# Start bytes of TensorE's operands in the second layer, and a first chunk of 510 columns

## The chip, the core and the metric

The kernel runs on one core of a Trainium2 chip. The metric is the time of one execution on the device in microseconds; the text gives the median of several runs and, for its reasoning, the one execution that the profiler recorded.

## What is computed

The reference takes x (2 x 3008 x 256), makes the real part of its Fourier transform over the last two axes, and sends the 6016 rows through two layers, each with its own weights of 256 x 2048 and 2048 x 256:

```
X = fft(fft(x, axis=1), axis=2).real              # 6016 rows of 256
h = X @ w_in;  g = h * sigmoid(h);  y = g @ w_out                # layer one
h = y @ w_in2; g = h * clip(h + 3, 0, 6) / 6; out = g @ w_out2   # layer two
```

## The kernel before, in words

The transform comes first, as three steps of small matmuls (function names step1, step2, step3). Because x is real, rows come in pairs: a pair of rows is one column of a table `eo` that holds the even and the odd part, and there are 3010 pairs (`NPAIR`, 2 x 1505). The table is cut along its columns into six **chunks** (lines 52 to 56): the first has 512 columns, the other five 500 each, together `NCOL` = 3012. The last two columns are padding; line 429 sets them to zero. All that follows is done chunk by chunk, so a matmul streams 500 or, in the first chunk, 512 columns.

**Precision.** Every product in float32 is made of three matmuls on float32r halves (`mm3`, lines 302 to 305): the high half of the weights times the high half of the moving operand (line 303), high times low (line 304), low times high (line 305). Each matmul has a weight load of its own. So weights exist as `whi` and `wlo`, hidden values as `ghi` and `glo`, and so on.

**Layer one** (`win1`, `win1_end`, `wout1`). For each chunk and each of 16 blocks of 128 hidden units: two products into `ab` (6 matmuls) and four products into the accumulators `y` (12 matmuls), 18 matmuls in all. The two layers' outputs between them go to DRAM (`y1_d`) and come back as `u`.

**Layer two** (the loop over `units2` at the end of `body`). The first product of the layer is done with seven products in place of eight on pairs of blocks. The seven moving operands are made by `moving` from `u`, in this order: b11, b21, t1, t2, t4, t3, b22. The seven products are at lines 888, 889, 897, 910, 923, 925 and 939; in the profile they read `pa<-b` (b11), `pc<-b` (b21), `pb<-t` (t1), `pa<-t,wx` (t2), `pd<-t` (t4), `pa<-t,whi` (t3) and `pb<-b` (b22). The weights of b11, b21, t4 and t3 come from `whi` and `wlo`, those of t1, t2 and b22 from `wx`, sums of weights that `load_w2` (line 264) loads. Then `wout2` makes eight products into `y`. A unit is one pair of blocks of a chunk: 7 x 3 + 8 x 3 = 45 matmuls; a chunk has eight units. Chunk 1 has its pass between the two halves of chunk 0, chunks 2 to 5 follow, and a product's accumulation runs a little behind.

**Where operands lie.** Every operand tile has rows of 512 words (`LINE`), so each half starts at the same byte modulo 512 as its tile; only the number of columns streamed differs. The tiles come from pools at these addresses (bytes in a partition):

- weights of both layers (`wp`, from 8,448 on): 256 modulo 512
- hidden values `ghi`, `glo` (right side of the memory): 448
- the ring of operands (line 687): 10 slots, `x0` to `x9`. Slots 0 to 3 lie in `xsp`, on the right side (from 184,256 on): 448. Slots 4 to 9 lie in `xq` (line 615; from 114,944 on): 256. The counter starts at slot 4, and each pass takes seven slots in the order of the operands above. Chunk 0 is taken twice, so the passes are chunk 0, 1, 0, 2, 3, 4, 5.
- `wx` (line 266): it takes the place of `eo` at 204,736: 448

In layer one moving operands lie in `xsp` (448) and weights in `wp` (256). Right-side pools are laid from the top of the memory downwards; the topmost slot is the one that `eo` and `wx` share, 24,608 bytes, set by the larger of the two.

The order of the work is written out by hand in `body`: the program order on each engine is the order of the calls. Loads and stores go through SP's queue, some stores of layer one through POOL's.

Of the kernel before, what the change touches and what calls it, by code (L numbers as in the profile page):

```python
# [36 lines left out]
F32 = mybir.dt.float32  # L37
F32R = mybir.dt.float32r
# [8 lines left out]
NPAIR = B * (S // 2 + 1)  # L47
SELF = NB // 2 + 1
HALFB = NPAIR // B
FF, P = 2048, 128  # L50
NF = FF // P
NCOL = 3012
CHUNK = 512
LINE = 512
CHUNKS = [(max(0, 500 * j + 12), 500) for j in range(6)]
CHUNKS[0] = 0, CHUNK


NJ = NB // 4
# [24 lines left out]
def body(tc, xh, x128, t1, t2, t3, w1, w128, w2, out):  # L84
    nc = tc.nc
    V, A, T, G = nc.vector, nc.scalar, nc.tensor, nc.gpsimd
# [4 lines left out]
    eop = tc.alloc_tile_pool(name="eop", bufs=1, side="right")  # L91
# [3 lines left out]
    three, mask, minus, warm = (consts[:, i : i + 1] for i in range(4))  # L95
    eo = eop.tile([P, 2, NCOL], F32, name="eo", tag="eo")
    w2_d = [
        [dr.tile([P, 2, n], F32, name=f"w2{q}_d{g}", tag=f"w2{q}_d{g}") for q, n in (("h", 512), ("l", 512), ("x", 384))]
        for g in range(NF // 2)
    ]  # L100
    e128_d = [dr.tile([1, n], F32, name=f"e128_d{j}", tag=f"e128_d{j}") for j, (_, n) in enumerate(CHUNKS)]
    x_d = [[dr.tile([P, 2, n], F32, name=f"x{h}_d{j}", tag=f"x{h}_d{j}") for h in "hl"] for j, (_, n) in enumerate(CHUNKS)]
    y1_d = [dr.tile([P, 2, 2 * n], F32, name=f"y1_d{j}", tag=f"y1_d{j}") for j, (_, n) in enumerate(CHUNKS)]

# [34 lines left out]
    def weight_tiles(key, g):  # L139
        whi[key, g] = wp.tile([P, 2, 512], F32R, name=f"whi{key}_{g}", tag=f"whi{g}")  # L140
        wlo[key, g] = wp.tile([P, 2, 512], F32R, name=f"wlo{key}_{g}", tag=f"wlo{g}")
# [69 lines left out]
    wx = []  # L211
# [51 lines left out]

    def load_w2(g):
        if not wx:
            flat = eop.tile([P, NF * 384 + 8], F32R, name="wx", tag="eo")[:, : NF * 384]
            wx.append(flat.rearrange("p (g i c) -> p g i c", i=2, c=384))
        weight_tiles(2, g)
        for dst, src in zip((whi[2, g], wlo[2, g], wx[0][:, g]), w2_d[g]):
            nc.sync.dma_start(dst.bitcast(F32), src)  # L270
# [155 lines left out]
        return c + 256  # L426

    V.memset(three, 3.0)
    V.memset(eo[:, :, NPAIR:], 0.0)
    G.memset(nil, 0.0)  # L430
    cleared = (V, ((2, 0, 1), (2, 2, 3), (3, 0, 2))), (G, ((2, 1, 2), (2, 3, 4), (3, 2, 4), (4, 0, 4), (5, 0, 4)))
    for eng, slots in cleared:
# [74 lines left out]
    def split_eo(k, j):  # L507
        c, n = CHUNKS[j]
        hi, lo = (xsp.tile([P, 2, LINE], F32R, name=f"x{h}{k}", tag=f"x{2 * (k % 2) + i}") for i, h in enumerate(("hi", "lo")))
        eb = xsp.tile([P, LINE], F32, name=f"eb{k}", tag="eb", bufs=2)  # L510
        new = k < len(CHUNKS)
        if new:
            nc.sync.dma_start(e128_d[j], eo[0:1, 1, c : c + n])
        nc.sync.dma_start(eb[:, :n], e128_d[j].to_broadcast([P, n]))
        if new:
            split(hi[:, :, :n], lo[:, :, :n], eo[:, :, c : c + n], x_d[j])
        else:
            for x, d in zip((hi, lo), x_d[j]):
                nc.sync.dma_start(x[:, :, :n].bitcast(F32), d)
        return hi, lo, eb  # L520
# [93 lines left out]
    stp = tc.alloc_tile_pool(name="stp", bufs=1, reuse_waits="tile")  # L614
    xq = tc.alloc_tile_pool(name="xq", bufs=1, reuse_waits="tile")
    psB = tc.alloc_tile_pool(name="psB", bufs=1, space=PSUM, reuse_waits="tile")
    kept, ys = {}, {}

    def low(k, f, shared=False):
# [129 lines left out]
    for i in range(n1):  # L749
        k, f = units[i]  # L750
        j, fs = segs[k]
# [29 lines left out]
        if not odd and 0 <= q < FIRST + 1:  # L781
            load_w2(q)
# [92 lines left out]
    for e, (k, f) in enumerate(units2):  # L875
        j, fs = segs2[k]
# [64 lines left out]
        if e < half - FIRST - 1:  # L941
            load_w2(FIRST + 1 + e)
# [146 lines left out]
```

## Time and profile before

| | |
|---|---|
| median of 3 runs | 923.89 us (923.83 to 923.91) |
| the profiled execution | 923.64 us |
| its span, first to last instruction | 921.5 us |
| PE busy, share of the span | 915.9 us, 99% |
| DVE, ACT, POOL busy | 661.9, 649.6, 527.3 us |
| matmuls | 4286 |

PE is TensorE's matmuls, PEld its weight loads, DVE VectorE, ACT ScalarE, POOL GpSimd, SP the queue of SyncE. Matmuls are pipelined: a recorded duration reaches from a matmul's start to its modelled end and overlaps the next one, so what counts on PE is the distance from one start to the next.

### The profile page before, as it was taken

How to read it: one execution, taken by the hardware profiler on the slowest of the kernel's cores; microseconds unless marked ns; L12 is line 12 of the kernel's file. 1: busy time of each engine (PE TensorE's matmuls, PEld its weight loads, DVE VectorE, ACT ScalarE, POOL GpSimd, SP SyncE). 2: the span in 40 equal slices, each digit the busy share in tenths (PEclk: the TensorE clock that was granted, in tenths of full speed). 3: DMA queues.
4: the chain of work that ended last, by engine and by line, in shares of the span. 5: the costliest groups of instructions: out<-in, count | busy, mean ns of one | idle time of the engine just before them, and what ended most of it. 6: DMA issues, size and time to landing. Idle time of an engine off the chain costs nothing.

```text
span 921.5 us, 12152 instructions
## 1 busy us (share of the span) xinstructions
PE 915.9 (99%) x4286; PEld 775.2 (84%) x4286; DVE 661.9 (72%) x908; ACT 649.6 (70%) x1144; POOL 527.3 (57%) x391
## 2 busy tenths in 40 slices
PE   9999999999999999999999999999999999999998
PEld 8988888888888888888888888888888888888886
DVE  7989999989899999985564565565555555555544
ACT  4878767666767666677776778666776777677665
POOL 2065646745465665554775577745765675576553
PEclk9999999999999999999999999999999999999999
DMA  8554344043272726696230002020020002001001
GB/s 323 195 209 158 136 146 143 6 143 145 85 207 92 220 93 163 188 371 198 107 90 1 1 1 90 0 91 1 1 90 0 1 1 90 1 1 45 1 1 44
DMA packets 28744, 89.32 MB, mean 97 GB/s; under 512 B 2886, under 2 KB 14667, under 8 KB 25644
## 3 DMA queue, kind: packets, MB, share of 16 engines
q1 hardware_dynamic: 26796, 81.85, 24.9%
q0 software_dynamic: 1504, 6.17, 3.7%
q8 instruction: 33, 0.54, 0.2%
q10 hardware_dynamic: 384, 0.54, 0.2%
q14 instruction: 27, 0.22, 0.1%
HBM read 52.33 MB, written 36.22 MB: 96 GB/s over the span
## 4 chain that ended last, share of the span: by engine, by line
PE 98%; DVE 1%; DMA 0%; ACT 0%; issue 0%; SPq 0%
PE y L303 18%; PE y L304 18%; PE y L305 18%; PE ab L303 5%; PE ab L304 5%; PE ab L305 4%; PE pa L303 4%; PE pa L304 4%; PE pa L305 4%; PE pb L305 2%; PE pb L303 2%; PE pb L304 2%; PE ps L368 1%; PE ps L411 1%; PE pd L304 1%; PE pc L303 1%
## 5 line engine op out<-in xcount | busy, mean ns | idle before, releaser
L806 POOL TENSOR_TENSOR glo<-h,ghi 128x500 fp32r<-128x500 f32 (+1 forms) x191 | 246.4, 1302 | 186.7 <-ACT ghi L803 182.7
L624 POOL TENSOR_TENSOR glo<-h,ghi 128x500 fp32r<-128x500 f32 (+1 forms) x137 | 211.8, 1559 | 190.9 <-ACT h L583 182.3
L303 PE MATMUL y<-ghi,whi 128*128 128x500 f32 (+1 forms) x768 | 295.7, 385 | 0.0
L304 PE MATMUL y<-glo,whi 128*128 128x500 f32 (+1 forms) x768 | 295.6, 385 | 0.0
L305 PE MATMUL y<-ghi,wlo 128*128 128x500 f32 (+1 forms) x768 | 295.4, 385 | 0.0
L303 PEld LDWEIGHTS y<-ghi,whi 128*128 128x128 f32 x768 | 144.3, 188 | 27.3
L305 PEld LDWEIGHTS y<-ghi,wlo 128*128 128x128 f32 x768 | 144.2, 188 | 27.0
L304 PEld LDWEIGHTS y<-glo,whi 128*128 128x128 f32 x768 | 144.2, 188 | 26.9
L803 ACT ACTIVATE ghi<-h 128x500 fp32r<-128x500 f32 (+1 forms) x192 | 118.0, 624 | 47.9 <-DVE h L798 46.6
L582 ACT ACTIVATE ghi<-ab 128x500 fp32r<-128x500 f32 (+1 forms) x96 | 56.4, 587 | 87.2 <-DVE h L573 85.4
L798 DVE SCALAR_TENSOR_TENSOR h<-h,pc 128x500 f32<-128x500 f32 (+1 forms) x96 | 65.1, 678 | 71.5 <-ACT h L795 71.5
L928 DVE TENSOR_TENSOR pc<-u,pb 128x500 f32<-128x500 f32 (+1 forms) x48 | 32.9, 685 | 109.5 <-ACT u L864 109.5
L795 ACT ACTIVATE h<-pc,consts 128x500 f32<-128x500 f32 (+1 forms) x96 | 64.6, 673 | 40.4 <-DVE pc L928 36.0
L864 ACT ACTIVATE u<-pa 128x500 f32<-128x500 f32 (+1 forms) x96 | 56.6, 589 | 51.7 <-PE pa L305 48.4
L303 PE MATMUL ab<-xhi,whi 128*128 128x500 f32 (+1 forms) x192 | 74.4, 387 | 0.2 <-DVE st L562 0.2
L304 PE MATMUL ab<-xlo,whi 128*128 128x500 f32 (+1 forms) x192 | 74.0, 386 | 0.0
L305 PE MATMUL ab<-xhi,wlo 128*128 128x500 f32 (+1 forms) x192 | 73.8, 384 | 0.0
L562 DVE SCALAR_TENSOR_TENSOR st<-eb,w_sb,ab 128x500 f32<-128x500 f32 (+1 forms) x92 | 67.0, 728 | 8.3 <-PE ab L305 8.3
L573 DVE SCALAR_TENSOR_TENSOR h<-st,ab 128x500 f32<-128x500 f32 (+1 forms) x92 | 61.3, 667 | 7.8 <-PE ab L305 7.7
L798 DVE SCALAR_TENSOR_TENSOR h<-h,pd 128x500 f32<-128x500 f32 (+1 forms) x96 | 64.4, 671 | 1.2 <-ACT h L795 1.2
L795 ACT ACTIVATE h<-pd,consts 128x500 f32<-128x500 f32 (+1 forms) x96 | 64.6, 673 | 0.5 <-DVE pd L940 0.5
L583 ACT ACTIVATE h<-h 128x500 f32<-128x500 f32 (+1 forms) x96 | 60.0, 625 | 3.0
(166 smaller groups left out, 1576.2 us busy)
## 6 DMA issues: line engine op xcount, KB each, us to landing
raw<-in_w SPq DMA_DIRECT2D x16, 1024.0 KB, 6.9
y_d<-st SPq DMA_DIRECT2D x5, 1000.0 KB, 5.1
y_d<-st POOLq DMA_DIRECT2D x5, 1000.0 KB, 8.0
u<-y_d SPq DMA_DIRECT2D x5, 1000.0 KB, 5.3
out<-st SPq DMA_DIRECT2D x19, 250.0 KB, 2.2
w2h_d<-h SPq DMA_DIRECT2D x8, 512.0 KB, 2.6
w2l_d<-t SPq DMA_DIRECT2D x8, 512.0 KB, 3.2
whi<-w2h_d SPq DMA_DIRECT2D x8, 512.0 KB, 5.8
```

What stands on the lines that cost most here:

```text
L303: T.matmul(o, wh, xhi, start=first, stop=False, **group)
L304: T.matmul(o, wh, xlo, start=False, stop=False, **group)
L305: T.matmul(o, wl, xhi, start=False, stop=last, **group)
L562: V.scalar_tensor_tensor(out=z[:, :n], in0=eb[:, :n], scalar=w128_sb[:, f : f + 1], in1=ab[:, :n], op0=ALU.mult, op1=ALU.add)
L573: V.scalar_tensor_tensor(out=h[:, 0, :n], in0=z[:, :n], scalar=2.0, in1=ab[:, :n], op0=ALU.mult, op1=ALU.subtract)
L583: A.activation(h[:, s, :n], src, AF.Silu)
L624: eng.tensor_tensor(out=glo[:, s, :n], in0=h[:, s, :n], in1=ghi[:, s, :n], op=ALU.subtract)
L795: A.activation(h[:, i, :n], c[:, :n], AF.Relu, bias=three)
L798: V.scalar_tensor_tensor(out=h[:, i, :n], in0=h[:, i, :n], scalar=6.0, in1=c[:, :n], op0=ALU.min, op1=ALU.mult)
L803: A.activation(g[0][:, i, :n], h[:, i, :n], AF.Copy)
L806: E.tensor_tensor(out=g[1][:, i, :n], in0=h[:, i, :n], in1=g[0][:, i, :n], op=ALU.subtract)
L864: A.activation(t[:, :n], pa[:, :n], AF.Copy)
```

## The change

The chunks cover exactly the 3010 pairs: the first has 510 columns in place of 512, the others begin two columns earlier, and the padding and its memset go. The slot of `wx` gets 128 words more, and `wx` starts 80 words (320 bytes) into it. A tile of 48 words (192 bytes) that nobody uses stands at the head of `xq`.

```
-NCOL = 3012
+NCOL = 3010
 CHUNK = 512
 LINE = 512
-CHUNKS = [(max(0, 500 * j + 12), 500) for j in range(6)]
-CHUNKS[0] = 0, CHUNK
+CHUNKS = [(max(0, 500 * j + 10), 500) for j in range(6)]
+CHUNKS[0] = 0, 510
...
     def load_w2(g):
         if not wx:
-            flat = eop.tile([P, NF * 384 + 8], F32R, name="wx", tag="eo")[:, : NF * 384]
+            flat = eop.tile([P, NF * 384 + 136], F32R, name="wx", tag="eo")[:, 80 : 80 + NF * 384]
...
     V.memset(three, 3.0)
-    V.memset(eo[:, :, NPAIR:], 0.0)
     G.memset(nil, 0.0)
...
     psB = tc.alloc_tile_pool(name="psB", bufs=1, space=PSUM, reuse_waits="tile")
+    xq.tile([P, 48], F32, name="gap", tag="gap")
```

## Rows read from the trace of the kernel before

**Rows 1.** The page, its first lines: the span, and each engine's busy time.
```profile
span 921.5 us, 12152 instructions
## 1 busy us (share of the span) xinstructions
PE 915.9 (99%) x4286; PEld 775.2 (84%) x4286; DVE 661.9 (72%) x908; ACT 649.6 (70%) x1144; POOL 527.3 (57%) x391
```
**Rows 2.** The page, the chain that ended last, shares of the span by engine.
```profile
PE 98%; DVE 1%; DMA 0%; ACT 0%; issue 0%; SPq 0%
```
**Rows 3.** Waits of PE, longest: us in total, times, longest us.
```profile
PE psw L351 <- POOL nil L430: 1.0, 1, 1.0
```
**Rows 4.** Windows in layer 2: length, then busy us (records that overlap) by engine.
```profile
core 0: us, PE busy (x) PEld busy (x) DVE busy (x) ACT busy (x) POOL busy (x), PEclk, DMA share, GB/s
481.80:549.00 67.20, 67.20 (x304) 56.70 (x303) 36.49 (x58) 46.99 (x80) 38.78 (x30) 1.00 0.01 5
603.80:671.20 67.40, 67.40 (x304) 56.84 (x303) 38.08 (x60) 46.54 (x79) 38.52 (x30) 1.00 0.07 24
```
**Rows 5.** Timeline of PE in layer 1: start us, duration us; eight matmuls between.
```profile
300.02 0.38 PE L304 MATMUL ab<-xlo,whi 128*128 128x500 f32 x1
...
302.00 0.38 PE L304 MATMUL y<-glo,whi 128*128 128x500 f32 x1
```
**Rows 6.** Groups by form, 260 to 370 us (layer 1): busy us, mean ns | idle.
```profile
L303 PE MATMUL y<-ghi,whi 128*128 128x500 f32 x112 | 42.8, 382 | 0.0
```
**Rows 7.** Groups by form, 671.2 to 751.2 us (layer 2, chunk 3).
```profile
L304 PE MATMUL y<-glo,whi 128*128 128x500 f32 x64 | 24.6, 384 | 0.0
...
L304 PE MATMUL pd<-t,whi 128*128 128x500 f32 x8 | 3.1, 390 | 0.0
...
L304 PE MATMUL pc<-b,whi 128*128 128x500 f32 x8 | 3.1, 382 | 0.0
```
**Rows 8.** Groups by form, 831 to 911 us (layer 2, chunk 5).
```profile
L304 PE MATMUL pc<-b,whi 128*128 128x500 f32 x8 | 3.1, 390 | 0.0
...
L304 PE MATMUL pd<-t,whi 128*128 128x500 f32 x8 | 3.1, 382 | 0.0
```
**Rows 9.** Timeline of PE in layer 2: starts at the edges of passes.
```profile
481.67 0.38 PE L303 MATMUL pb<-t,wx 128*128 128x500 f32 x1
...
549.13 0.39 PE L303 MATMUL pa<-b,whi 128*128 128x512 f32 x1
...
603.73 0.39 PE L303 MATMUL pb<-t,wx 128*128 128x500 f32 x1
...
671.26 0.39 PE L303 MATMUL pa<-b,whi 128*128 128x500 f32 x1
...
751.19 0.39 PE L303 MATMUL pa<-b,whi 128*128 128x500 f32 x1
...
830.98 0.39 PE L303 MATMUL pa<-b,whi 128*128 128x500 f32 x1
...
910.95 0.39 PE L303 MATMUL y<-ghi,whi 128*128 128x500 f32 x1
```
**Rows 10.** Groups by form, whole span: matmuls of 512 columns.
```profile
L305 PE MATMUL y<-ghi,wlo 128*128 128x512 f32 x128 | 50.6, 396 | 0.0
L303 PE MATMUL y<-ghi,whi 128*128 128x512 f32 x128 | 50.6, 395 | 0.0
...
L304 PE MATMUL pa<-t,whi 128*128 128x512 f32 x8 | 3.2, 398 | 0.0
...
L303 PE MATMUL pa<-t,whi 128*128 128x512 f32 x8 | 3.1, 390 | 0.0
```
**Rows 11.** Groups by form, around 173 us: the first and second 512-wide matmul after 500-wide ones.
```profile
L304 PE MATMUL ab<-xlo,whi 128*128 128x512 f32 x1 | 0.4, 398 | 0.0
L303 PE MATMUL ab<-xhi,whi 128*128 128x512 f32 x1 | 0.4, 387 | 0.0
```
**Rows 12.** Timeline of DVE at the start: start us, duration us, [idle before].
```profile
0.85 0.06 DVE L429 MEMSET eo<- 128x4 f32 x1
...
4.17 0.43 DVE L339 TENSOR_TENSOR x<-x 128x256 f32<-128x256 f32 x1 [0.82 <-DMA x<-in_xh]
```
**Rows 13.** DMA issues: KB each, median us to landing.
```profile
out<-st SPq DMA_DIRECT2D x4, 256.0 KB, 2.1
```

## The prediction

> **What bounds the kernel now.** I read the page's engine shares first, then the chain, then the waits of PE. PE is busy 915.9 of 921.5 us, the chain that ends last is PE for 98% of it, and the longest single wait of PE in the whole run is 1.0 us at the start [rows 1, 2, 3]. So the time is the sum of the steps from one matmul's start to the next, and everything else runs beside it. A change can pay here only by fewer matmuls, narrower ones, or a shorter step for the same width.
>
> The windows by stage show the other engines: in a 67.4 us stretch of layer 2 ACT is busy 46.5 us, POOL 38.5 and DVE 38.1, with the granted clock at 1.00, the 2.4 GHz level [rows 4]. None of them is near PE.
>
> Now the step itself. The timeline of a layer-1 stretch has starts at 300.02 and, nine matmuls later, at 302.00: 0.220 us a step for 500 columns [rows 5]. The same matmuls are listed with a duration of 382 ns [rows 6]: durations overlap, so I read a row's step as its duration less 162 ns. In layer 1 every row of that stretch says 382.
>
> In layer 2 they don't, and the rows tell why. Take two passes with the same code, weights and width. From 671 to 751 us the product pd (operand t4) takes 390 ns and pc (operand b21) 382 [rows 7]; from 831 to 911 us it is the other way round, pd 382 and pc 390 [rows 8]. What differs is the slot of the operand. The ring starts at slot 4 and takes seven slots a pass, so in the first of these passes b21 is in slot 3 (xsp, byte 448 of 512) and t4 in slot 6 (xq, byte 256); in the second b21 is in slot 7 (xq) and t4 in slot 0 (xsp). Their weights lie at 256. A product whose operand and weights start at the same byte of 512 is slow; one with 448 against 256 is not. Neighbours pay as well: y, always 448 against 256, is at 384 in this pass and at 382 in layer 1 [rows 6, 7].
>
> **The change, part by part.** *Layer 2, 500 columns.* The 48-word tile puts xq at 114,944 + 192 = 115,136, which is 448 modulo 512. The slot of wx grows from 24,608 to 25,120 bytes, so the pools of the right side all move down by 512 and keep their 448, and wx starts at 204,224 + 320 = 204,544, which is 256. Then every matmul of layer 2 has the pairing of layer 1, and I give it layer 1's 0.220 us. What this removes comes from starts. A unit has 45 matmuls, a pass of eight units 360. From 671.26 to 910.95 are three passes: 239.69 us against 1080 x 0.220 = 237.60, an excess of 2.09 [rows 9]. From 481.67 to 549.13 and from 603.73 to 671.26 there are 303 each (the windows list 304, one of which began earlier [rows 4]): 67.46 and 67.53 against 66.66, an excess of 0.80 and 0.87 [rows 9]. That is 3.76 us over 1686 matmuls; the other 114 of the 1800 are mixed with wider ones, and at the same rate hold 0.25. **Term: -4.0 us**, with 3.5 to 4.3 as its bounds (without the 114, and less some that stays at the joints; or a little more at the joints).
>
> *First chunk, 510 columns.* It has 16 x 18 = 288 matmuls in layer 1 and 360 in layer 2. At 512 columns y and ab have about 395.4 ns, a step of 233.4; the 168 products of layer 2 lie between 398 and 390, about 393, a step of 231 [rows 10]. So here the pairing hardly matters. And width is not smooth: the first 512-wide matmul after a run of 500 takes 387, just 5 ns for 12 columns (0.42 ns each), but the next one 398 [rows 11]. No row has 510. From below, it is 220 + 10 x 0.42 = 224.2 a step, if a run of 510 stays on that first step. From above, it is the costliest of 512, 398 - 162 = 236. I take the nearest row, 512, less two columns: 233.4 - 0.8 = 232.6. For 288 + 192 matmuls that is 0.8 ns less, -0.40 us; for the 168 products, which now all have the other pairing and which I let go to the same 232.6, +0.27. **Term: -0.13 us**, between -5.6 (480 x 9.2 + 168 x 6.8 ns) and +2.1 (480 x 2.6 + 168 x 5.0 ns).
>
> *The rest.* The memset of the padding is 0.06 us on DVE, which afterwards waits 0.82 us for the first input anyway [rows 12]: nothing; without that cover 0.06 us. The first chunk's transfers lose two columns in 512 (its stores of 256 KB land in 2.1 us, on SP's queue [rows 13]); PE waits for no DMA in either layer, so nothing. No step is moved, no wait is added. If PE gets faster, the next engine in layer 2 is ACT, busy for 46.5 of 67.4 us [rows 4], and 303 steps of 0.220 still take 66.7: nothing becomes late.
>
> **Sum.** -4.0 - 0.13 = -4.13 on the profiled execution of 923.64 us (span 921.5 and 2.1 around it): 919.5. The median of the runs is 0.25 above the profiled one, so 919.8.
>
> **Rivals.** *The first chunk goes cheap.* With 510 columns the step stays near 224.2 to 229. For: the lone 512-wide matmul at 387. Against: every longer run of 512 is 8 ns above that. By its end the time is 923.9 - 4.0 - 5.6 = 914.3. The Trainium skill, "TensorE: Matmul & The Clock Gate", section Back-to-back issue gap, has the gap grow by one cycle per column, so by that page this rival would hold; the row at 387 agrees with it, and the rows at 395 do not.
>
> *Addresses are not the cause.* Something else that differs between the passes makes the 390s, and only two columns in 648 matmuls go: 648 x 0.83 ns = 0.54 us, 923.35, no measurable change. Against: pd and pc swap places exactly with their slots. The Trainium skill, "SBUF — State Buffer", section Who interferes with whom, gives PE two independent read ports, one for the moving operand and one for weights, and says that "PE and ACT never wait on anyone"; by that page the start bytes could not matter and this rival would hold. The rows with 390 and 382 for one line speak against it.
>
> *Slower: 510 is a bad width.* 510 columns are 2,040 bytes, no multiple of 16, where 500 and 512 are. If each such matmul pays another step of the size that the rows show between 387 and 398, it is 648 x 11 ns = 7.1 us: 923.9 - 4.0 + 7.1 = 927.0. It decides from 4.0 / 648 = 6.2 ns a matmul on. For: the price of width is visibly uneven. Against: no row shows an odd price for a width that isn't a multiple of something.
>
> *The layout doesn't come out as stated*, say wx is moved but the ring is not: then products only trade places, and the time stays at about 923. Against: the addresses above follow from the tile sizes.
>
> **Chances.** Forecast (first chunk between 229 and 236 a step) 0.66; cheap first chunk 0.20; addresses not the cause 0.07; bad width 0.04; layout 0.03. A change of 0.2%, 1.85 us, is about what a measurement can tell. The forecast and the cheap chunk lie below 922.04, but for the forecast's last edge; so faster 0.85, same 0.10, slower 0.05. The range takes the two ends of the unknown width, 914.3 to 923.9 - 4.0 + 2.1 = 922.0; it leaves out the last three cases, 0.14.
>
> **What would show it.** Right: from the second chunk on, all products of layer 2 and y at 382 in every pass, and three passes in 237.6 us. For the first chunk, rows of 510 near 394 to 395; 386 to 387 means the cheap rival, above 400 the bad width. Wrong: pd or pc still at 390 in some pass, or layer-2 steps that lengthen with new waits of PE on ACT or DVE.

## The result, and the profile after

The changed kernel takes 916.35 us (median of 4 runs, 916.08 to 916.56) against 923.9 before: a ratio of 0.9918, 95% interval 0.9901 to 0.9935, 7.55 us less. The profiled execution took 916.08 us, its span is 914.0 [before: rows 1]. The text had forecast 919.8 with a range of 914.3 to 922.0.

The page's first lines after. PE is still the whole span; it has the same 4286 matmuls.
```profile
span 914.0 us, 12150 instructions
## 1 busy us (share of the span) xinstructions
PE 908.0 (99%) x4286; PEld 774.4 (85%) x4286; DVE 664.1 (73%) x907; ACT 649.6 (71%) x1144; POOL 528.3 (58%) x391
```
Groups by form of the whole span: first the 500-wide `y`, then `y` and two products of the first chunk, now 510 wide.
```profile
L303 PE MATMUL y<-ghi,whi 128*128 128x500 f32 x640 | 244.5, 382 | 0.0
...
L304 PE MATMUL y<-glo,whi 128*128 128x510 f32 x128 | 49.8, 389 | 0.0
...
L304 PE MATMUL pa<-t,whi 128*128 128x510 f32 x8 | 3.1, 389 | 0.0
...
L303 PE MATMUL pa<-t,whi 128*128 128x510 f32 x8 | 3.1, 388 | 0.0
```
The same view for the pass of chunk 3, 665.8 to 745 us, where pd and pc had changed places with their slots [rows 7, 8]:
```profile
L304 PE MATMUL pc<-b,whi 128*128 128x500 f32 x8 | 3.1, 382 | 0.0
...
L304 PE MATMUL pd<-t,whi 128*128 128x500 f32 x8 | 3.1, 382 | 0.0
```
And the timeline of PE at the first and last edge of the three last passes [rows 9]:
```profile
665.84 0.38 PE L303 MATMUL pa<-b,whi 128*128 128x500 f32 x1
...
903.44 0.38 PE L303 MATMUL y<-ghi,whi 128*128 128x500 f32 x1
```
The three passes take 903.44 - 665.84 = 237.60 us, exactly 1080 steps of 0.220, where they took 239.69. In these passes the excess of layer 2 at 500 columns is gone as forecast. The first chunk is the surprise: its rows stand at 389, a step of 227, where 512 columns had 395 and the forecast 394 to 395.

A little was given back. Around the start of the pass of chunk 1 some steps are long. The timeline of PE, two places:
```profile
466.23 0.38 PE L305 MATMUL pa<-b,wlo 128*128 128x500 f32 x1
466.49 0.50 PE L303 MATMUL pc<-b,whi 128*128 128x500 f32 x1
466.83 0.39 PE L304 MATMUL pc<-b,whi 128*128 128x500 f32 x1
...
470.70 0.39 PE L303 MATMUL pd<-t,whi 128*128 128x500 f32 x1
471.02 0.50 PE L304 MATMUL pd<-t,whi 128*128 128x500 f32 x1
471.36 0.39 PE L305 MATMUL pd<-t,wlo 128*128 128x500 f32 x1
```
Steps of 0.26, 0.34, 0.32 and 0.34 us in place of 0.22 are 0.4 us in these four alone. What PE waited for there stands in the timelines of DVE and POOL:
```profile
465.75 0.69 DVE L798 SCALAR_TENSOR_TENSOR h<-h,pc 128x510 f32<-128x510 f32 x1 [0.22 <-ACT h L795]
...
469.68 2.50 POOL L693 TENSOR_TENSOR t<-u,t 128x500 fp32r<-128x500 f32 x2
```
The matmul at 466.49 overwrites pc, which DVE had read until 466.44. The one at 471.02 takes the low half of t4, the first of the two that POOL made from 469.68 on; it was done just before. Over all long steps from 465 to 476 us the excess is 0.67 us, where the same work had 0.20 in the kernel before.

### The profile page after: what moved, and what is told of

The parts are those of the page before. It is cut to its first block, busy times and chain, and to the rows that moved or that the text cites. A ratio compares the mean times of both kernels' runs of the same rounds, so it can differ in the third digit from the quotient of the medians.

```text
span 914.0 us, 12150 instructions
## 1 busy us (share of the span) xinstructions
PE 908.0 (99%) x4286; PEld 774.4 (85%) x4286; DVE 664.1 (73%) x907; ACT 649.6 (71%) x1144; POOL 528.3 (58%) x391
## 4 chain that ended last, share of the span: by engine, by line
PE 98%; DVE 1%; DMA 0%; ACT 0%; issue 0%; SPq 0%
PE y L305 18%; PE y L303 18%; PE y L304 18%; PE ab L303 5%; PE ab L304 5%; PE ab L305 5%; PE pa L303 3%; PE pa L305 3%; PE pa L304 3%; PE pb L303 2%; PE pb L304 2%; PE pb L305 2%; PE ps L368 1%; PE ps L411 1%; PE pd L304 1%; PE pc L303 1%
```

## The experiments

**The two parts alone.** e1 has the new addresses with the old chunks, e2 the new chunks with the old addresses.

```
 e1 (against the changed kernel)
-NCOL = 3010
+NCOL = 3012
-CHUNKS = [(max(0, 500 * j + 10), 500) for j in range(6)]
-CHUNKS[0] = 0, 510
+CHUNKS = [(max(0, 500 * j + 12), 500) for j in range(6)]
+CHUNKS[0] = 0, CHUNK
...
+    V.memset(eo[:, :, NPAIR:], 0.0)

 e2 (against the changed kernel)
-            flat = eop.tile([P, NF * 384 + 136], F32R, name="wx", tag="eo")[:, 80 : 80 + NF * 384]
+            flat = eop.tile([P, NF * 384 + 8], F32R, name="wx", tag="eo")[:, : NF * 384]
...
-    xq.tile([P, 48], F32, name="gap", tag="gap")
```

> The operand addresses of the change, with the chunks of before (first chunk 512 columns with its padding). Theory: the two parts are separate, and the addresses give 4.0 us in layer 2 at 500 columns (every row there at 382 ns), while the 512-wide products lose some 0.4 us since they go to the 233 ns step of the others; about 920.3 us. Rival: the addresses give the whole gain, by way of the first chunk too: about 916.4. Second rival: the gain needs the new width: about 923.

> First chunk of 510 columns, operand addresses as before. Theory: layer 1 at 510 columns steps by 226.7 ns in place of 233, 1.8 us less; in layer 2 the 500-wide rows keep 382 to 390 ns, and the 510-wide ones lie between 226.7 and 231 ns, 0.5 to 2.0 us less; 920.1 to 921.6 us. Rival: the 510 columns run at 226.7 only with the new addresses: about 923.4.

e1 took 920.68 us, a ratio of 0.9966 (0.9955 to 0.9977); e2 920.74, 0.9964 (0.9951 to 0.9977). So each part gives 3.3 us against 923.99 in the same runs; together 6.6, against 7.55 for both at once, which is within the intervals. The rows by form of `y` in e1 say which width each had:
```profile
L303 PE MATMUL y<-ghi,whi 128*128 128x500 f32 x640 | 244.6, 382 | 0.0
...
L303 PE MATMUL y<-ghi,whi 128*128 128x512 f32 x128 | 50.5, 395 | 0.0
```
And in e2, with a product that still takes turns between the two kinds of slot:
```profile
L303 PE MATMUL y<-ghi,whi 128*128 128x500 f32 x640 | 245.1, 383 | 0.0
...
L303 PE MATMUL y<-ghi,whi 128*128 128x510 f32 x128 | 49.8, 389 | 0.0
...
L304 PE MATMUL pd<-t,whi 128*128 128x500 f32 x40 | 15.6, 389 | 0.0
```
The parts are nearly separate: the addresses bring 500-wide rows to 382 and leave the 512-wide `y` at 395; the new width brings `y` to 389 with either layout. Part of what is missing to 7.55 is in the first chunk's products: in e1 the 512-wide ones go from about 393 to 395, and in e2 the 510-wide ones keep 388 to 393, where the change has nearly all at 389. Another part has nothing to do with either: in the profiled executions of e1 and e2 the transform ends 0.33 us later than before and in the change (first matmul of the chunks at 44.14, against 43.80 and 43.81).

**What about the addresses counts?** All operands and weights were put on one pairing of start bytes for both layers, by padding the pools: a tile of some words ahead of the weights, another length of the gap, another start of `wx`. e3 is the pairing that looked slow; e7, e8, e9 and e10 move the weights only; e12 turns the pairing of the change round.

```
 e3: per.tile([P, 48], F32, name="pad") after consts; wx and xq as before the change
 e7:  pad 32 words, gap 16, wx from word 112   (moving 448, weights 384)
 e8:  pad 112, gap 64, wx from word 64         (moving 448, weights 192)
 e9:  pad 64, gap 112, wx from word 16         (moving 448, weights 0)
 e10: pad 16, gap 32, wx from word 96          (moving 448, weights 320)
 e12: pad 48, gap 80, wx slot NF * 384 + 56, from word 48   (moving 256, weights 448)
```

> Chunks of the change, but every moving operand and every weight of both layers starts at 448 modulo 512: one pairing throughout, the one that looked slow. Theory (equal start bytes cost by themselves): rows of 500 columns at 386 to 390 ns in both layers, 4 to 8 ns on 3240 matmuls, 13 to 26 us more than the changed kernel: 929 to 942 us. Rival (only the passage from one pairing to another costs): rows of 382 ns, 916 to 918 us.

> Chunks of the change; moving operands at 448 modulo 512 in both layers as in the change, all weights at 384 in place of 256, so 64 bytes apart in place of 192. Theory (only equal start bytes cost): rows of 500 columns at 382 ns, 916 to 917 us. Rival (it takes a distance of more than 64): rows at 386 to 389 ns as with equal bytes, 929 to 938 us.

> Chunks of the change; moving operands at 448 modulo 512 in both layers, all weights at 192 in place of 256, so 256 bytes apart, half of 512. Theory (only equal start bytes modulo 512 cost): rows of 500 columns at 382 ns, 916 to 917 us. Rival (the unit is 256 bytes, not 512): rows at 386 to 389 ns, 929 to 938 us.

> Chunks of the change; moving operands at 448 modulo 512 in both layers, all weights at 0 in place of 256. Theory (the unit is 256 bytes, since the pairing 448 with 192 ran row for row like 448 with 448): this is the pairing of the change shifted by one unit, so 500-wide steps at 220 and 510-wide ones at 226.7 as there, 916 to 917 us. Rival (the unit is 512 and 448 with 256 is a single good pairing): 500-wide steps at 226 to 227, 936 to 941 us.

> Chunks of the change; moving operands at 448 modulo 512 in both layers, all weights at 320, 128 bytes apart. Theory (192 is the one good distance of the four in a unit of 256, since 0 and 64 are slow): 500-wide steps at 226 to 227, 936 to 941 us. Rival (from 128 on it is free): steps at 220, 916 to 917 us.

> Chunks of the change; the pairing of the change the other way round in both layers: every moving operand at 256 modulo 512, every weight at 448. Theory (the pair of bytes counts and either order is good, as the short groups of 256 with 448 before the change suggest, which ran at 220 to 221 ns a step): 500-wide steps at 220, 916 to 917 us. Rival (the distance from weights to moving operand counts, taken modulo 256: it is 64 here, and 64 was slow): 500-wide steps at 226 to 227, 936 to 941 us.

The times (one run each, but for the change), and the distance from the weights' start to the moving operand's, modulo 256:

| | moving, weights | distance | us |
|---|---|---|---|
| the change | 448, 256 | 192 | 916.35 |
| e9 | 448, 0 | 192 | 916.57 |
| e3 | 448, 448 | 0 | 937.53 |
| e8 | 448, 192 | 0 | 936.57 |
| e7 | 448, 384 | 64 | 940.63 |
| e12 | 256, 448 | 64 | 940.50 |
| e10 | 448, 320 | 128 | 940.09 |

Groups by form of `y` over the whole span, e9, 500 and 510 columns:
```profile
L303 PE MATMUL y<-ghi,whi 128*128 128x500 f32 x640 | 244.5, 382 | 0.0
...
L303 PE MATMUL y<-ghi,whi 128*128 128x510 f32 x128 | 49.8, 389 | 0.0
```
The same of e8 (e3 has 389 and 389 too):
```profile
L304 PE MATMUL y<-ghi,whi 128*128 128x500 f32 x640 | 248.7, 389 | 0.0
...
L304 PE MATMUL y<-ghi,whi 128*128 128x510 f32 x128 | 49.8, 389 | 0.0
```
And of e12 (e7 has the same two means):
```profile
L304 PE MATMUL y<-ghi,whi 128*128 128x500 f32 x640 | 249.1, 389 | 0.0
...
L304 PE MATMUL y<-ghi,whi 128*128 128x510 f32 x128 | 50.2, 392 | 0.0
```
In e3 `y`, whose own pairing was a good one before, goes to 389, so a slow pairing costs by itself, and about 20 us when all matmuls have it. But the theory that only equal bytes cost fell with e7 and e8: 64, 128 and 256 apart are as slow. What holds over all seven is the distance modulo 256: kernels with the same distance agree in their rows, whichever the single bytes are, and of 0, 64, 128 and 192 only 192 is fast at 500 columns. e12 was the sharpest: the two bytes of the change the other way round make 64, and it runs like e7. These seven times alone would also fit the weights' byte by itself: the two fast kernels are those with weights at 0 modulo 256. The kernel before rules that out: there the weights of pd lie at 256 in both passes, and pd takes 390 with its operand at 256 and 382 with it at 448 [rows 7, 8]. Distances between these four were not tried.

**What about the width counts?** Chunks of other widths, with the addresses of the change; one run each.

```
 e4: CHUNKS = [(max(0, 502 * j + -2), 502) for j in range(6)];  CHUNKS[0] = 0, 500
 e5: widths 508, 506, 504, 498, 494, 500, one chunk after the other
 e6: widths 492, 488, 486, 484, 482, 480
```

> Addresses of the change; chunks of 500 and five times 502 columns in place of 510 and five times 500. Theory (the step goes in jumps of 6.7 ns, and 500 is the last width on its level): 502-wide rows at 389 ns, 3240 x 6.7 ns more, first chunk 648 x 6.7 ns less: about 933.7 us. Rival (0.42 ns for each column, up to some width below 510): 502-wide rows at 383 ns, 3240 x 0.8 ns more and 4.3 us less: about 914.8 us.

> Addresses of the change; six chunks of 508, 506, 504, 498, 494 and 500 columns (3010 in all). Theory (the step has levels, 220 up to 500 and 226.7 from 502 to 510): rows of 494, 498 and 500 columns at 382 ns, rows of 504, 506 and 508 at 389; three chunks on each level, 3 x 648 x 220 + 3 x 648 x 226.7 ns, two chunks more on the upper level than the changed kernel, 8.7 us: about 925 us. Rival (widths that are multiples of four run better): 504 and 508 at 382 to 384, 498 and 494 at 386 to 389.

> Addresses of the change; six chunks of 492, 488, 486, 484, 482 and 480 columns. It leaves out the last 98 of the 3010 column pairs. Theory (levels of 16 columns, the next boundary below 500 is 484): rows of 484, 482 and 480 at 375 to 376 ns (a step of 213.3), rows of 486, 488 and 492 at 382 (220); about 3 x 648 x 6.7 = 13 us less than six chunks at 220, some 899 us. Rival (500 is a single lucky width and below it the step falls evenly by 0.42 ns a column): rows falling from 379 to 374 by twos; about 902 us.

e4 took 934.01 us, as the first theory had it: two columns more cost a whole jump. The row by form of its 502-wide `y`:
```profile
L303 PE MATMUL y<-ghi,whi 128*128 128x502 f32 x640 | 248.9, 389 | 0.0
```
e5 took 933.19, and both of its theories missed. Its rows of `y`:
```profile
L302 PE MATMUL y<-ghi,whi 128*128 128x506 f32 x128 | 50.2, 392 | 0.0
L302 PE MATMUL y<-ghi,whi 128*128 128x508 f32 x128 | 50.0, 391 | 0.0
L302 PE MATMUL y<-ghi,whi 128*128 128x504 f32 x128 | 49.9, 390 | 0.0
L302 PE MATMUL y<-ghi,whi 128*128 128x498 f32 x128 | 49.6, 387 | 0.0
L302 PE MATMUL y<-ghi,whi 128*128 128x500 f32 x128 | 49.0, 383 | 0.0
L302 PE MATMUL y<-ghi,whi 128*128 128x494 f32 x128 | 48.9, 382 | 0.0
```
e6 took 907.6, and missed too; it leaves out the last 98 of the 3010 pairs, so only its rows count, not its time. The rows of its ends:
```profile
L302 PE MATMUL y<-ghi,whi 128*128 128x492 f32 x128 | 48.9, 382 | 0.0
...
L302 PE MATMUL y<-ghi,whi 128*128 128x484 f32 x128 | 48.9, 382 | 0.0
...
L302 PE MATMUL y<-ghi,whi 128*128 128x482 f32 x128 | 48.8, 381 | 0.0
L302 PE MATMUL y<-ghi,whi 128*128 128x480 f32 x128 | 48.3, 378 | 0.0
```
There are no even levels and no rule of four. From 484 to 494 columns the row is flat at 382; 498 and 502 are dearer than 500 between them; 506 and 508 are dearer than 510. 500 and 510 are good points of an uneven curve, and 512, at 395, the worst of all. Only 500, 510 and 512 were run at other distances than 192; whether another width is good there is open.

**The steps given back.** e11 moves some low halves of chunk 1's operands from POOL to DVE.

```
-            (V if k == 0 and name in ("b21", "t2", "t3") else G).tensor_tensor(out=lo, in0=src, in1=hi, op=ALU.subtract)
+            (V if k <= 1 and name in ("b21", "t2", "t3") else G).tensor_tensor(out=lo, in0=src, in1=hi, op=ALU.subtract)
```

> The changed kernel with one edit: the low halves of b21, t2 and t3 are made on DVE in place of POOL for the second pass of layer two also, as for the first. Theory (in the changed kernel seven matmuls between 465 and 476 us wait for a low half from POOL, 0.7 us over their steps in all, against two and 0.2 us before): those long steps go but for one or two, span 0.4 to 0.7 us below the 914.0 of the changed kernel, about 915.8 us. Rival (the wait is for DVE or ACT, ahead of POOL): long steps stay or move, 916 to 917 us.

It took 917.00 us, 0.9922 (0.9906 to 0.9939): no gain. The long steps at t2, t3 and t4 went, but a new wait came ahead of them, longer than what they cost. With PE that much later, the operands would have been ready in any case, so e11 does not show POOL as the cause. For t4 the trace of the changed kernel shows it; the long step at t3 there follows a copy by ACT that ended at 472.21, and the one at t2 stays open. The steps at b21, where PE waits for DVE, stayed. The timeline of PE and DVE around the new wait in e11:
```profile
468.71 0.77 DVE L693 TENSOR_TENSOR t<-u,t 128x500 fp32r<-128x500 f32 x1 [1.21 <-ACT t L689]
...
469.40 0.68 DVE L940 TENSOR_TENSOR pd<-u,pb 128x510 f32<-128x510 f32 x1
...
470.14 0.50 PE L303 MATMUL pb<-t,wx 128*128 128x500 f32 x1 [0.89 <-DVE pd L940]
```
DVE now waits for ACT to make the high half of t3; the sum at line 940, which reads pb, is queued behind that, and PE waits 0.89 us for it to give back pb. Span 915.2 against 914.0. No version here that computes all 3010 pairs beats the changed kernel.

## Why the prediction was right, and where it was off

**The bound** was right: almost nothing but steps of PE changed, and the time followed their sum.

**Layer 2 at 500 columns**, -4.0 us: right. The last three passes run at 0.220 throughout. e1 alone gives 3.3 us; with the 0.33 us that its transform lost, and some 0.3 that the 512-wide products lost (168 at about 2 ns), that is 3.9.

**The rule behind it** was half right. "A product whose operand and weights start at the same byte of 512 is slow; one with 448 against 256 is not": the second half holds for an operand at 448 and weights at 256, and not the other way round (e12). In the first, equal bytes are only one of the slow distances, and the unit is 256. The trace of before misled in one point: groups of 256 against 448 (t1, t2 and b22 with `wx`) stood at 382 in their own rows, and the slow ones were those after them. Two more rows of the kernel before, groups by form of 671.2 to 751.2 us: t1, and b11, which has the good pairing but follows b22:
```profile
L304 PE MATMUL pa<-b,whi 128*128 128x500 f32 x8 | 3.1, 388 | 0.0
...
L304 PE MATMUL pb<-t,wx 128*128 128x500 f32 x8 | 3.1, 382 | 0.0
```
e12 shows that this pairing held throughout is at 389. A group of three matmuls is too short to show its price in its own row; "neighbours pay as well" should have made the text doubt it.

**The first chunk**, -0.13 us, is the term that was mis-sized. "I take the nearest row, 512, less two columns: 232.6" failed: 510 columns step at 389 - 162 = 227. With the rows of before, 480 x 233.4 + 168 x 231 ns = 150.8 us, and after 648 x 227 ns = 147.1: -3.7 us. That lies between the stated bounds, -5.6 and +2.1, and inside what the text called the cheap rival (0.20), not the case that it held likeliest (0.66). None of the signs that the prediction named fits 389: they were 394 to 395, 386 to 387, and above 400. The nearest row in columns was no guide, since the cost of width is uneven (e4, e5, e6); a straight line from 500 to 512 would have given 393. The time fell inside the stated range because the range took in both ends of the unknown width, not because the sum had the width right.

**Nothing becomes late** was wrong by about half a microsecond (0.67 against 0.20): at the joint to chunk 1's pass PE came early, and waited for DVE to give back pc and for POOL's low half of t4. Chunk 1's operands are prepared during the four units of the first chunk before it, and these went faster; that this is why is argued, not shown. The busy shares of a whole pass, which the text used, don't show such a joint.

**The sum.** -4.0 - 3.7 = -7.7, some 0.5 given back: -7.2, against 7.5 in the spans and 7.55 in the medians.

**The pages.** The Trainium skill, "SBUF — State Buffer", section Who interferes with whom, has PE's two read ports independent and PE waiting on no one; by that page e3 would have run like the changed kernel, and it took 21 us more; why is not shown. The Trainium skill, "TensorE: Matmul & The Clock Gate", section Back-to-back issue gap, has one cycle per column, but for an isolated matmul, a condition that the prediction left out. Here 500 to 502 columns cost 6 to 7 ns a matmul, and 484 to 494 nothing.

## What to carry to other kernels

Where PE is the whole span and every matmul has its own weight load, look at the mean duration of the same line by pass: a few nanoseconds that move with a buffer's slot are worth a layout change. Hold one pairing of start bytes for all matmuls and measure the distance modulo 256 and the width together, in a long run of equal matmuls; neighbouring widths and short groups tell little. In float32r here, 500 columns with a distance of 192 bytes were the best of those tried, per column.

## What the runs showed that was not expected

The distance of start bytes modulo 256 sets the step: 220 ns at 192, 227 at 0, 64 and 128, for 500 columns. The step is not monotonic in the width: 382 ns recorded at 494, 387 at 498, 383 at 500, 389 at 502, 392 at 506, 389 at 510, 395 at 512. In the kernel before, the first 512-wide matmul after 500-wide ones took 387, and the next 398 [rows 11]: a change of width is paid a matmul late. Why the step depends on start bytes and width in this way is open; the runs show the dependence, not its mechanism.
